# One DMA transpose per ds tile, and ten single ds buffers, in the backward loop of a fused attention and FFN kernel

## The chip, the cores and the metric

The kernel runs on one core of one Trainium2 chip. The metric is the device time of one execution in microseconds (us); lower is better. Most executions of one kernel lie within 0.3% of their median. "Ratio" is always the mean time of one kernel's fast runs over that of the kernel before in the same rounds on the same chip, so it is not quite the ratio of the medians that stand beside it.

## The reference, cut to what matters

The function is a transformer block with attention and a SwiGLU FFN in parallel; the kernel returns its output and the gradients of the input and of five weights.

```
xn  = layernorm(x)                                   # x: 2048 x 448, 16 heads of 28
out = x + attention(xn, wqkv, wo) + swiglu(xn, w_gate, w_up, w_down)
grads = vjp(out)(grad_out)
```

The attention backward needs, for every head and every tile of 128 queries by 512 keys, the matrix ds (the softmax weights times the gradient that reaches them). ds is used as it is for dk, and transposed for dq. How it gets transposed is what the change is about.

## The kernel before

The backward loop has 512 steps; a step treats one query tile of two heads. Four steps, qi = 0 to 3, make a block. In each step TensorE (PE) computes two score tiles and two gradient tiles, ScalarE (ACT) the exponentials and VectorE (DVE) the two products that are ds. In a block, the tiles 0 and 1 are transposed by one DMA as a pair, tile 2 by a DMA of its own, and tile 3 by PE. All these DMAs and, but for four stores at its start, all loads and stores of the loop are issued by SyncE (SP), one after the other.

```python
def dst_dma(b, ds, qi):                       # transposes by DMA, issued on SP
    if qi == 2:
        SP.dma_start_transpose(out=dsT[b][:, 2]..., in_=ds[:, 0]...)        # 8 tiles of 128 x 128
        return
    dsT[b] = bk.tile([P, 4, 2, 4, P], BF16, name="dsT", bufs=3)
    SP.dma_start_transpose(out=dsT[b][:, 0:2]..., in_=ds[:]...)             # 16 tiles: the pair

def ew(k):
    ...                                       # ACT: e_sb = exp(scores)
        if qi % 2 == 0:
            dss[k - 1] = dss[k] = kq.tile([P, 2, 2, 512], BF16, name="ds_sb", bufs=5)   # a pair
        ds = dss[k - 1]
        for j in range(2):
            DVE.tensor_tensor(out=ds[:, qi % 2, j], in0=dps.pop((k - 1, j))[:], in1=est[k - 1][:, j], op=ALU.mult)
        if qi == 1 or qi == 2 and b < NB // 4 - 1:
            ... dst_dma(b, ds, qi)

def tr_unit(b):                               # tile 3 by PE, at step 4b + 8
    ds = dss.pop(4 * b + 3)
    ...
def dq_unit(b):                               # PE, at step 4b + 13: reads dsT[b], all four tiles
    ...
def flush(upto):                              # stores of the loop, also on SP
    while held and held[0][0] <= upto:
        _, o, i = held.pop(0)
        SP.dma_start(out=o, in_=i)

for k in range(NB + 12):                      # cut
    row(k); ew(k)                             # PE rows, then ACT and DVE
    flush(k); drop()                          # stores due, loads due
    ...                                       # dk/dv matmuls, tr_unit, dq_unit, fill-in matmuls
```

A ds pair lives in one of five buffers, so DVE may start to rewrite it nine steps after the pair was complete, if its readers are done; the last of them is often the DMA transpose.

The softmax here doesn't subtract the row's maximum and nothing guards it: scores larger than these inputs give would overflow.

## Time and profile before

Runs gave a median of 1472.74 us (1466.82 to 1473.25).

| | us |
|---|---|
| span of the profiled execution | 1468.9 |
| backward loop (first ds product to the last, worked out from the trace) | 801.1 |
| PE idle in the loop (neither a matmul nor a weight load) | 52.3 |
| DVE waiting for a ds transpose | 15.9 |
| SP's issue time in the loop: 255 transposes | 561 |
| SP's issue time in the loop: 283 other DMAs (plain, but for one transpose of another tile) | 167 |

From the page of the kernel before: the span; busy time of the engines; and the group of the ds products (line, engine, operation, shapes, count, then busy us and mean ns, then idle us before it).

```profile
span 1468.9 us, 34341 instructions
...
PE 1338.7 (91%) x12647; PEld 544.8 (37%) x12708; DVE 1153.9 (79%) x1997; ACT 1262.4 (86%) x2193; POOL 361.8 (25%) x486
...
L845 DVE TENSOR_TENSOR ds_sb<-db,e_sb 128x512 bf16<-128x512 f32 x1024 | 648.4, 685 | 68.6 <-PE db L818 22.6
...
DMA packets 697664, 271.14 MB, mean 185 GB/s; under 512 B 616128, under 2 KB 672152, under 8 KB 697496
```

No engine is far ahead of the others, so a stall of any of them soon holds up PE. From the tile view of dsT: engine, operation and count of the two kinds of transpose, with shortest, median and longest duration of their issue in ns.

```profile
L830 SPq DMA_TRANSPOSE dsT<-ds_sb x128: 1746/3044/4773, 626.8 to 1419.8; - x128
...
L826 SPq DMA_TRANSPOSE dsT<-ds_sb x127: 1232/1252/2486, 629.8 to 1415.9; - x127
```

A pair keeps SP for 3.0 us in the median, but 1.75 at best. The timeline of SP (start, us, what it issued) in a bad stretch shows that SP never pauses:

```profile
657.27 1.43 SPq L800 DMA_DIRECT2D out_dram<-dqT  x2
658.80 2.03 SPq L826 DMA_TRANSPOSE dsT<-ds_sb  x1
660.92 0.52 SPq L800 DMA_DIRECT2D dqkvT_d<-dkv  x1
661.50 0.97 SPq L767 DMA_DIRECT2D h_c<-F_d  x2
662.57 3.27 SPq L830 DMA_TRANSPOSE dsT<-ds_sb  x1
665.88 1.06 SPq L800 DMA_DIRECT2D out_dram<-dqT  x2
667.04 1.24 SPq L826 DMA_TRANSPOSE dsT<-ds_sb  x1
```

The pair issued at 662.57 had been ready since 653.85 (the end of its last ds product): SP is 8.7 us late with it. It landed at 667.69, and the DVE timeline of the same stretch (in brackets: idle time before the instruction and what ended it) shows who had been waiting for that buffer:

```profile
662.79 2.52 DVE L845 TENSOR_TENSOR ds_sb<-db,e_sb 128x512 bf16<-128x512 f32 x4 [0.67 <-DMA dsT<-ds_sb]
667.82 2.49 DVE L845 TENSOR_TENSOR ds_sb<-db,e_sb 128x512 bf16<-128x512 f32 x4 [2.51 <-DMA dsT<-ds_sb]
```

The waits view adds these up (us in total, times, longest): DVE for the transposes, and PE for DVE.

```profile
PE db L818 <- DVE ds_sb L845: 18.7, 36, 2.7
...
DVE ds_sb L845 <- DMA dsT<-ds_sb: 15.9, 11, 2.5
```

### The profile page before, as it was taken

To read this page: it belongs to the slowest core of one execution; us is meant where nothing else is said; L and a number is where in the kernel's file an instruction comes from. 1 tells how busy PE (TensorE), PEld (TensorE's weight loads), DVE (VectorE), ACT (ScalarE), POOL (GpSimd) and SP (SyncE) were. 2 spreads that over 40 slices of the span, in tenths; PEclk is the share of its full clock that TensorE was granted. 3 is DMA by queue.
4 is the path that set the end of the run, shared out by engine and by line. 5 is a ranking of instruction groups with operands and counts; after the bars stand their busy time and mean duration, and the time that the engine had idled before them with its cause. 6 is when DMAs were issued, how large, how long until landed. Compare 5 with 4: busy or idle time off the path is not lost. (4 is left out here: it accounts for less than half of the span.)

```text
span 1468.9 us, 34341 instructions
## 1 busy us (share of the span) xinstructions
PE 1338.7 (91%) x12647; PEld 544.8 (37%) x12708; DVE 1153.9 (79%) x1997; ACT 1262.4 (86%) x2193; POOL 361.8 (25%) x486
## 2 busy tenths in 40 slices
PE   5889999989999999888899989999999999999996
PEld 2333333333333333333333433433343444344343
DVE  6667756656667767497888878888889999899988
ACT  5789988988989998687888879899989999888974
POOL 6464514553344444010001101101001011010005
PEclk9999999999999999998999999999999999999998
DMA  5797957696778685699999999999999999999961
GB/s 151 147 210 179 223 118 179 165 197 155 167 160 190 145 184 125 206 198 199 214 204 196 214 204 189 210 203 216 212 195 194 206 217 217 199 194 206 193 140 59
DMA packets 697664, 271.14 MB, mean 185 GB/s; under 512 B 616128, under 2 KB 672152, under 8 KB 697496
## 3 DMA queue, kind: packets, MB, share of 16 engines
q1 hardware_dynamic: 692520, 262.82, 86.7%
q0 software_dynamic: 3568, 5.83, 1.8%
q8 instruction: 100, 1.64, 0.5%
q14 instruction: 68, 0.56, 0.1%
q10 hardware_dynamic: 1408, 0.30, 0.1%
HBM read 65.04 MB, written 59.90 MB: 85 GB/s over the span
## 5 line engine op out<-in xcount | busy, mean ns | idle before, releaser
L845 DVE TENSOR_TENSOR ds_sb<-db,e_sb 128x512 bf16<-128x512 f32 x1024 | 648.4, 685 | 68.6 <-PE db L818 22.6
L837 ACT ACTIVATE e_sb<-sb 128x512 bf16<-128x512 f32 x1024 | 554.1, 609 | 60.3 <-PE db L818 43.8
L611 ACT ACTIVATE eT<-s_w 128x1024 bf16<-128x1024 f32 x256 | 263.7, 1030 | 48.6 <-PE s_ps L608 45.8
L613 ACT ACTIVATE eT<-s_ps 128x512 bf16<-128x512 f32 x512 | 280.2, 611 | 0.0
L818 PE MATMUL db<-kd,qd 32*128 32x512 bf16 x1024 | 239.9, 385 | 19.5 <-DVE ds_sb L845 18.7
L810 PE MATMUL sb<-kd,qd 32*128 32x512 bf16 x1024 | 210.9, 389 | 7.5 <-DMA qd<-QD_d 3.7
L964 POOL TENSOR_TENSOR dq_acc<-dq_acc,dq_st 128x256 f32<-128x256 f32 x64 | 46.4, 724 | 588.6 <-ACT dq_st L962 588.6
L905 ACT COPY dsT<-db 128x1024 bf16<-128x1024 bf16 x128 | 130.0, 1016 | 37.1 <-PE db L900 36.5
L922 PE MATMUL acc<-ds_sb,qd 128*32 128x512 bf16 x1024 | 161.4, 392 | 0.0
L918 PE MATMUL acc<-e_sb,qd 128*32 128x512 bf16 x1024 | 159.4, 392 | 1.3 <-DVE dw_o L527 1.3
L379 POOL TENSOR_TENSOR nn<-nn,ag 128x512 f32<-128x512 f32 x56 | 71.2, 1272 | 253.9 <-DVE ag L377 245.4
L608 PE MATMUL s_ps<-QQ,KK 32*128 32x512 bf16 x512 | 125.5, 385 | 3.9
L1132 PE MATMUL genb<-wguT,dau_c 128*128 128x448 bf16 x448 | 117.5, 355 | 6.3 <-ACT dq_st L962 3.8
L608 PE MATMUL s_w<-QQ,KK 32*128 32x512 bf16 x512 | 100.3, 387 | 13.2 <-ACT eT L611 10.2
L810 PEld LDWEIGHTS <-qd 32*128 32x128 bf16 x1024 | 48.3, 91 | 152.6 <-issue 140.6
L420 PE MATMUL gen<-xn_t,f_sp 128*128 128x448 bf16 x416 | 91.8, 354 | 2.6 <-DVE nn L394 1.7
L949 PE MATMUL genb<-dsT,kd 128*32 128x256 bf16 x2048 | 80.9, 279 | 3.5 <-DVE y L1084 1.8
L420 PEld LDWEIGHTS <-f_sp 128*128 128x128 bf16 x640 | 55.7, 98 | 76.4 <-issue 31.7
L900 PE MATMUL db<-ident_bf,ds_sb 128*128 128x128 bf16 x1032 | 82.1, 225 | 0.9 <-DVE ds_sb L845 0.9
L900 PEld LDWEIGHTS <-ds_sb 128*128 128x128 bf16 x1032 | 70.6, 101 | 28.6 <-issue 10.3
L450 PE MATMUL gen<-eT,VS 128*32 128x512 bf16 x1024 | 68.0, 382 | 6.0 <-DVE nn L394 3.8
L380 POOL TENSOR_TENSOR nn<-nn,tt 128x512 f32<-128x512 f32 x56 | 72.0, 1286 | 4.4
(163 smaller groups left out, 1872.0 us busy)
## 6 DMA issues: line engine op xcount, KB each, us to landing
F_d<-hda SPq DMA_DIRECT2D x56, 384.0 KB
dau_c<-F_d SPq DMA_DIRECT2D x56, 256.0 KB
h_c<-F_d SPq DMA_DIRECT2D x24, 256.0 KB
qd<-QD_d SPq DMA_DIRECT2D x24, 256.0 KB
dc<-dqkvT_d SPq DMA_DIRECT2D x12, 384.0 KB
dsT<-ds_sb SPq DMA_TRANSPOSE x255
wT_d<-wT_f SPq DMA_DIRECT2D x14, 256.0 KB
KD_d<-qk_sp SPq DMA_DIRECT2D x7, 512.0 KB
```

What stands on the lines that cost most here:

```text
L420: PE.matmul(ps[:, :D], lhsT=fsp[fc][:, t // 4, w, t % 4, :], rhs=rhs[:, t, :], start=(t == 0), stop=(t == NT - 1))
L608: PE.matmul(sp4[hh], lhsT=KK[g][r:r + HP, kt * P:(kt + 1) * P], rhs=QQ[g][r:r + HP, qsl], start=True, stop=True, tile_position=(r, 0))
L611: ACTE.activation(out=e2[0][:], in_=wide[:], func=ACT.Exp, scale=SCALE)
L613: ACTE.activation(out=e2[1][:, j], in_=sp4[2 + j], func=ACT.Exp, scale=SCALE)
L810: PE.matmul(s_ps[:], lhsT=qside[g, qc][r:r + HP, 0, qi * P:(qi + 1) * P], rhs=kside[g, kc][r:r + HP, 0, :], start=True, stop=True, tile_po ...
L818: PE.matmul(d_ps[:], lhsT=qside[g, qc][r:r + HP, 1, qi * P:(qi + 1) * P], rhs=kside[g, kc][r:r + HP, 1, :], start=True, stop=True, tile_po ...
L837: ACTE.activation(out=est[k][:, j], in_=sps.pop((k, j))[:], func=ACT.Exp, scale=SCALE)
L845: DVE.tensor_tensor(out=ds[:, qi % 2, j], in0=dps.pop((k - 1, j))[:], in1=est[k - 1][:, j], op=ALU.mult)
L900: PE.transpose(ps[:, c, :], ds[:, qi % 2, c // 4, (c % 4) * P:(c % 4 + 1) * P], ident_bf[:])
L905: ACTE.copy(out=o, in_=ps[:])
L918: PE.matmul(a[r:r + HP, :], lhsT=sp4[:, 1, r:r + HP], rhs=e[:, j, :], start=first, stop=last, tile_position=(0, r), skip_group_check=True)
L922: PE.matmul(a[r:r + HP, :], lhsT=sp4[:, 0, r:r + HP], rhs=ds[:, qi % 2, j, :], start=first, stop=last, tile_position=(0, r), skip_group_ch ...
```

## The change

Each of the tiles 0, 1 and 2 gets its own DMA transpose, issued as soon as DVE has made the tile, and ds is kept in ten buffers of one tile. The memory is the same. The core of the diff:

```diff
     def dst_dma(b, ds, qi):
-        if qi == 2:
-            SP.dma_start_transpose(out=dsT[b][:, 2]..., in_=ds[:, 0]...)
-            return
-        dsT[b] = bk.tile([P, 4, 2, 4, P], BF16, name="dsT", bufs=3)
-        SP.dma_start_transpose(out=dsT[b][:, 0:2]..., in_=ds[:]...)
+        if qi == 0:
+            dsT[b] = bk.tile([P, 4, 2, 4, P], BF16, name="dsT", bufs=3)
+        SP.dma_start_transpose(out=dsT[b][:, qi]..., in_=ds[:]...)
 ...
-            if qi % 2 == 0:
-                dss[k - 1] = dss[k] = kq.tile([P, 2, 2, 512], BF16, name="ds_sb", bufs=5)
-            ds = dss[k - 1]
+            ds = dss[k - 1] = kq.tile([P, 2, 512], BF16, name="ds_sb", bufs=10)
 ...
-            if qi == 1 or qi == 2 and b < NB // 4 - 1:
+            if qi < 2 or qi == 2 and b < NB // 4 - 1:
 ...                                          # readers index ds[:, j] in place of ds[:, qi % 2, j]
```

More of the change, by code (lines that the diff above doesn't have):

```diff
@@ L824, in dst_dma @@
     def dst_dma(b, ds, qi):
-        if qi == 2:
-            SP.dma_start_transpose(out=dsT[b][:, 2].rearrange("p j kt s -> p (j kt) s"),
-                                   in_=ds[:, 0].rearrange("p j k -> p (j k)"))
-            return
-        dsT[b] = bk.tile([P, 4, 2, 4, P], BF16, name="dsT", bufs=3)
-        SP.dma_start_transpose(out=dsT[b][:, 0:2].rearrange("p q j kt s -> p (q j kt) s"),
-                               in_=ds[:].rearrange("p q j k -> p (q j k)"))
+        if qi == 0:
+            dsT[b] = bk.tile([P, 4, 2, 4, P], BF16, name="dsT", bufs=3)
+        SP.dma_start_transpose(out=dsT[b][:, qi].rearrange("p j kt s -> p (j kt) s"),
+                               in_=ds[:].rearrange("p j k -> p (j k)"))
     def ew(k):
@@ L840, in ew @@
             b = (k - 1) // 4
-            if qi % 2 == 0:
-                dss[k - 1] = dss[k] = kq.tile([P, 2, 2, 512], BF16, name="ds_sb", bufs=5)
-            ds = dss[k - 1]
+            ds = dss[k - 1] = kq.tile([P, 2, 512], BF16, name="ds_sb", bufs=10)
             for j in range(2):
-                DVE.tensor_tensor(out=ds[:, qi % 2, j], in0=dps.pop((k - 1, j))[:], in1=est[k - 1][:, j], op=ALU.mult)
-            if qi == 1 or qi == 2 and b < NB // 4 - 1:
+                DVE.tensor_tensor(out=ds[:, j], in0=dps.pop((k - 1, j))[:], in1=est[k - 1][:, j], op=ALU.mult)
+            if qi < 2 or qi == 2 and b < NB // 4 - 1:
                 if bk is None:
@@ L895, in tr_unit @@
     def tr_unit(b):
-        ds = dss.pop(4 * b + 3)
         for qi in (3,) if b < NB // 4 - 1 else (2, 3):
+            ds = dss.pop(4 * b + qi)
             ps = ps_b.tile([P, 8, P], BF16, name="db", bufs=3)
             for c in range(8):
-                PE.transpose(ps[:, c, :], ds[:, qi % 2, c // 4, (c % 4) * P:(c % 4 + 1) * P], ident_bf[:])
+                PE.transpose(ps[:, c, :], ds[:, c // 4, (c % 4) * P:(c % 4 + 1) * P], ident_bf[:])
             o = dsT[b][:, qi].rearrange("p j kt s -> p (j kt) s")
@@ L913, in kv @@
         e = est.pop(k)
-        ds = dss[k] if qi == 3 else dss.pop(k)
+        ds = dss[k] if qi == 3 or k == NB - 2 else dss.pop(k)
         sp4 = qside[g, qc][:, 2:4, qi * P:(qi + 1) * P]
@@ L921, in kv @@
             r = HP * (2 * hp + j)
-            PE.matmul(a[r:r + HP, :], lhsT=sp4[:, 0, r:r + HP], rhs=ds[:, qi % 2, j, :],
+            PE.matmul(a[r:r + HP, :], lhsT=sp4[:, 0, r:r + HP], rhs=ds[:, j, :],
                       start=first, stop=last, tile_position=(0, r), skip_group_check=True)
@@ L1336, in dx_b @@
         ACTE.activation(out=t1, in_=ps, func=ACT.Identity, scale=rstd[:, t:t + 1], bias=sa)
-        t2 = kq.tile([P, 2, 512], FP32, name="ds_sb", bufs=5)[:, 0, :D]
+        t2 = kq.tile([P, 512], FP32, name="ds_sb", bufs=10)[:, :D]
         dy = dy2[t // 4][:, t % 4, :] if t < 8 else dy4[:, t - 8, :]
```

## The prediction

> # Prediction
>
> **What bounds the kernel now.** The change touches only the backward loop: 512 steps from about 620 to 1422 us of a 1468.9 us span, 1.57 us a step. In the windows view the engines are nearly level there: over 1000 to 1100 us PE 93.4, ACT 89.2, DVE 85.5 us busy.
>
> A hidden resource is the SP queue, which issues the DMAs. The tile view of dsT shows 128 transposes of a ds pair at a median 3.044 us of issue (1.746 to 4.773) and 127 of one ds tile at 1.252 us. Summing SP's DMA instructions in stretches of 50 us, it is issuing for 88 to 101% of the time from 650 to 1350 us. Pairs therefore leave late: from DVE's end of a pair to SP's start of its transpose pass 8 to 13 us at 660 to 700 us, about 8 us near 830 us, about zero after 1290 us. A ds buffer is rewritten nine steps (about 14 us) after its transpose could start, so where the lag is large DVE must wait: the waits view gives "DVE ds_sb <- DMA dsT" 15.9 us in 11 waits, half of it before 720 us. "PE db <- DVE ds_sb" (18.7 us) includes its echo.
>
> **What the change does.** Bytes, matmuls and DVE work stay. 128 pair issues become 256 single ones: 383 transposes instead of 255. A pair that found few DMAs outstanding took about 1.8 us, so two singles at 1.25 us cost SP about 0.7 us more there. With DMAs outstanding, pairs take 3.0 to 3.3 us, while a single right behind a pair mostly takes 1.25 us: I read the pair's extra time as waiting for room in the DMA rings, an inference. Two singles are then an estimated 2.5 to 3.1 us, 0 to 0.6 us less per four steps. The Trainium skill, page "DMA: Bandwidth & Descriptors", section "Rules for kernel authors", advises to coalesce small transfers; the unblocked case agrees (1.8 against 2.5 us), the blocked case need not.
>
> The first tile's transpose may start a step earlier, landing in about 3.5 us instead of 5.1 from issue, and every buffer has ten steps from that possible issue to its rewriting: 1.5 us more slack. Against this, a dsT buffer is claimed a step earlier, so the first transpose may wait on the dq matmuls three blocks back.
>
> **How much is critical.** Only the DVE waits on the transposes and their echo in PE: at most about 16 us (1.1%). I expect a third to a half to disappear and some to be given back where SP has more to issue: net about 4 us. Elsewhere a later landing is harmless: dq reads dsT about eleven steps after the tile was made.
>
> **Time:** 1468 us, 8 in 10 between 1450 and 1487. Faster by over 2%: 0.04; within 2%: 0.91; slower by over 2%: 0.05.
>
> **What would show it.** Tile view of dsT: 383 single issues, median 1.25 us; if blocking moves onto the second single, its mean is 1.5 us or more. Sum of transpose issue time: 561 us before, 480 to 590 after. Waits view: "DVE ds_sb <- DMA dsT" under 8 us. Groups view: DVE, ACT and PE busy within 1%. DMA packets and bytes unchanged.
>
> **What would make it wrong.** If each single keeps a ring wait, or 128 more instructions push SP past its capacity, lag rises everywhere and the time goes up by some per cent. If the lag lengthens steps (1.78 us around 700 us, 1.47 near 1150 us) beyond the waits credited to it, the gain could reach 25 us.

## The result, and the profile after

The changed kernel takes a median of 1451.63 us (1450.09 to 1452.04, 4 runs) against 1469.78 us (4 runs): ratio 0.9874, 95% interval 0.9843 to 0.9905. It is 1.3% faster, within the stated range but near its lower end; 4 us had been expected, 18 were measured.

The same lines of the page, of the changed kernel (its line 840 is line 845 of before):

```profile
span 1448.2 us, 34787 instructions
...
PE 1335.4 (92%) x12708; PEld 539.9 (37%) x12708; DVE 1151.7 (80%) x1997; ACT 1261.2 (87%) x2193; POOL 363.1 (25%) x486
...
L840 DVE TENSOR_TENSOR ds_sb<-db,e_sb 128x512 bf16<-128x512 f32 x1024 | 646.8, 684 | 54.7 <-issue 25.5
...
DMA packets 701763, 271.18 MB, mean 187 GB/s; under 512 B 620224, under 2 KB 676248, under 8 KB 701592
```

The work is the same on every engine; only idle time went. (The 61 matmuls that PE seems to have had fewer before are records missing from that trace, all of them ahead of the loop.) DVE's short gaps changed their label from "PE db" to "issue", not their size: 22.6 and 7.9 us before, 6.2 and 25.5 after, in the waits views. The waits that fell are those for the transposes. The tile view of dsT in the changed kernel:

```profile
L827 SPq DMA_TRANSPOSE dsT<-ds_sb x383: 1231/1267/3143, 624.3 to 1400.5; - x192
```

And its waits view:

```profile
PE db L818 <- DVE ds_sb L840: 6.4, 26, 0.6
...
DVE ds_sb L840 <- DMA dsT<-ds_sb: 5.0, 6, 1.7
```

SP's timeline in the same stretch shows loads and stores slipping in between single issues of 1.23 us, and some of 1.3 to 2.6 us:

```profile
657.14 1.23 SPq L827 DMA_TRANSPOSE dsT<-ds_sb  x1
658.43 0.57 SPq L767 DMA_DIRECT2D h_c<-F_d  x1
659.09 2.55 SPq L827 DMA_TRANSPOSE dsT<-ds_sb  x1
661.70 1.05 SPq L800 DMA_DIRECT2D out_dram<-dqT  x2
662.84 1.23 SPq L827 DMA_TRANSPOSE dsT<-ds_sb  x1
```

Of the 20.7 us between the two profiled spans, 16.7 lie in the loop (801.1 to 784.4); the rest (2.5 us ahead of the loop, where the code is the same, and 1.5 us in the tail) is within what runs differ by. The loop by stretches, worked out from the traces (loop time; SP's issue time on transposes; on plain DMAs; all in us; a stretch begins with the first ds product of its first step, so the sums differ by up to 2 us from the figures for the whole loop), with three of the experiments below beside the two kernels:

| | steps 0 to 159 | steps 160 to 319 | steps 320 to 511 |
|---|---|---|---|
| before | 264.0; 180.7; 65.4 | 249.3; 179.9; 52.0 | 288.5; 202.0; 48.4 |
| changed | 252.8; 164.2; 67.7 | 248.4; 175.5; 52.1 | 283.8; 206.1; 45.6 |
| e11: pairs, stores on POOL | 249.1; 184.4; 49.8 | 247.5; 191.5; 35.9 | 292.2; 213.3; 41.7 |
| e7: changed, tiny extra stores | 280.3; 159.8; 95.1 | 269.3; 168.7; 77.9 | 307.9; 198.3; 85.3 |
| e10: changed, stores on POOL | 250.6; 172.8; 57.8 | 246.0; 182.8; 36.8 | 283.8; 206.9; 39.7 |

Of the 16.7 us, 11.2 lie in the first 160 steps (8.9 in the control's profile), where SP has the most to issue for the time. SP is full there: its issue times and the short gaps between them (under 0.3 us) add up to 260 of the 264.0 us before, 250 of 252.8 after, 246 of 249.1 in e11 and 276 of 280.3 in e7. There its time on transposes fell by 16.5 us, or 0.41 us a block, of which the one more issue a block takes back some 0.1 us in a gap between issues. Over the whole loop the sum moved much less: 561 us before, 544 after, with some 13 us more of short gaps. So SP's time was saved just where it was short. The mean time from "ready" to "landed" fell from 8.9 us for a pair to 7.9 for its second tile, and the slowest tenth from over 13.9 to over 12.1 us, against the nine steps or 14.1 us after which a buffer was wanted again.

### The profile page after: what moved, and what is told of

Same layout as the page of the kernel before. It is cut to its first block, busy times and chain, and to the rows that moved or that the text cites. A ratio compares the mean times of both kernels' runs of the same rounds, so it can differ in the third digit from the quotient of the medians.

```text
span 1448.2 us, 34787 instructions
## 1 busy us (share of the span) xinstructions
PE 1335.4 (92%) x12708; PEld 539.9 (37%) x12708; DVE 1151.7 (80%) x1997; ACT 1261.2 (87%) x2193; POOL 363.1 (25%) x486
## 5 line engine op out<-in xcount | busy, mean ns | idle before, releaser
L840 DVE TENSOR_TENSOR ds_sb<-db,e_sb 128x512 bf16<-128x512 f32 x1024 | 646.8, 684 | 54.7 <-issue 25.5
L834 ACT ACTIVATE e_sb<-sb 128x512 bf16<-128x512 f32 x1024 | 555.0, 612 | 66.1 <-PE db L818 49.8
L818 PE MATMUL db<-kd,qd 32*128 32x512 bf16 x1024 | 236.1, 385 | 7.2 <-DVE ds_sb L840 6.4
L900 ACT COPY dsT<-db 128x1024 bf16<-128x1024 bf16 x128 | 130.2, 1017 | 14.1 <-PE db L895 13.5
L895 PE MATMUL db<-ident_bf,ds_sb 128*128 128x128 bf16 x1032 | 79.0, 220 | 1.1 <-DVE ds_sb L840 1.1
```

The lines of the kernel that those rows point to most:

```text
L818: PE.matmul(d_ps[:], lhsT=qside[g, qc][r:r + HP, 1, qi * P:(qi + 1) * P], rhs=kside[g, kc][r:r + HP, 1, :], start=True, stop=True, tile_po ...
L834: ACTE.activation(out=est[k][:, j], in_=sps.pop((k, j))[:], func=ACT.Exp, scale=SCALE)
L840: DVE.tensor_tensor(out=ds[:, j], in0=dps.pop((k - 1, j))[:], in1=est[k - 1][:, j], op=ALU.mult)
L895: PE.transpose(ps[:, c, :], ds[:, c // 4, (c % 4) * P:(c % 4 + 1) * P], ident_bf[:])
L900: ACTE.copy(out=o, in_=ps[:])
```

## The experiments

The change has three parts that could each be the cause: the granularity of the DMAs (theory G), the earlier start of the first tile's transpose (theory S), and the buffers (theory B). Behind G stands a further question, whether SP's time is what is scarce (theory Q) or whether a pair does harm whatever SP's load. "PE idle" and "loop" are worked out from each run's trace; "clock lost" is the span times (1 minus the mean granted TensorE clock), averaged over the fast runs. Runs were made on several chips; each ratio is to the kernel before on the same chip, where its median was 1469.50 us (a1, e1 to e3), 1467.83 (e7, e8), 1469.58 (e10) or 1469.61 (e11).

| run | median us | ratio (95%) | loop | PE idle | clock lost |
|---|---|---|---|---|---|
| before (11 runs beside the first four) | 1469.50 | 1 | 801.1 | 52.3 | 35.0 |
| changed, again (a1) | 1453.75 | 0.9892 (0.9875 to 0.9908) | 786.6 | 41.2 | 30.8 |
| e2: single DMAs, pair buffers | 1453.57 | 0.9890 (0.9872 to 0.9907) | 787.0 | 42.9 | 27.9 |
| e3: changed, both singles at the pair's time | 1454.35 | 0.9896 (0.9879 to 0.9913) | 787.1 | 41.7 | 28.0 |
| e1: pairs, six pair buffers | 1465.16 | 0.9972 (0.9958 to 0.9987) | 795.8 | 45.4 | 35.4 |
| e8: changed, twelve buffers | 1451.39 | 0.9873 (0.9847 to 0.9899) | 783.2 | 45.7 | 27.5 |
| e7: changed, 256 tiny extra stores | 1524.10 | 1.0383 (1.0358 to 1.0409) | 856.9 | 83.8 | 53.3 |
| e11: pairs, stores on POOL | 1453.55 | 0.9890 (0.9873 to 0.9906) | 788.1 | 47.5 | 24.7 |
| e10: changed, stores on POOL | 1443.81 | 0.9815 (0.9787 to 0.9844) | 779.7 | 40.1 | 24.1 |

### The control

> The changed kernel again, as the control on this chip for the other three. Every theory: 1450 to 1453 us, ratio to the kernel before 0.985 to 0.990. DVE waits on the transposes about 5 us in the waits view.

It came out as said: 1453.75 us. DVE's waits on the transposes were 3.1 us in its profile.

### Single DMAs from pair buffers

```diff
 # kernel before, dst_dma
-        if qi == 2: ...one tile...; else: ...the pair...
+        if qi == 0:
+            dsT[b] = bk.tile(...)
+        SP.dma_start_transpose(out=dsT[b][:, qi]..., in_=ds[:, qi % 2]...)
```

> The kernel before with its five pair buffers, but each tile of a pair transposed by its own DMA as soon as DVE has made it: the DMA half of the change alone. Theory G (granularity: single issues leave SP and land sooner because they do not stall on the DMA rings) expects nearly the whole gain, 1450 to 1456 us. Theory B (buffers: the gain is the extra step of slack and the separate release of ten buffers) expects little, 1464 to 1472 us. In between means both.

1453.57 us, the same as the changed kernel on the same chip. The DMA half of the change is all of it; the buffers add nothing that these runs can show.

### Both singles issued when the pair is complete

```diff
 # changed kernel, ew
-            if qi < 2 or qi == 2 and ...: dst_dma(b, ds, qi)
+            todo = [(dss[k - 2], 0), (ds, 1)] if qi == 1 else [(ds, 2)] if qi == 2 and ... else []
+            for d, q in todo: dst_dma(b, d, q)
```

> The changed kernel, but the first tile's transpose is issued only together with the second's, back to back, when the pair is complete. Theory G in its form 'two singles are cheaper than a pair whenever they leave' and theory B expect 1450 to 1455 us. Theory S (the gain is the earlier start of the first tile's transpose, which spreads the DMA work) expects most of the gain lost: 1462 to 1470 us.

1454.35 us. Two singles back to back, in the very place of the pair, keep the gain, so the earlier start is not the cause. Theory S falls. (e2 keeps the earlier start and e3 the finer buffers; no run here takes both away and keeps the single DMAs.) The two singles took 1.36 and 1.52 us of issue on average, 2.89 in sum against the pair's 3.01.

### Six pair buffers

```diff
-  ds_sb: bufs=5          # pairs
+  ds_sb: bufs=6          # gs and pr, scratch of the tail, moved into buffers of qd and kd, idle by then
```

> The kernel before with six pair buffers in place of five (room made by letting two scratch tiles of the tail, gs and pr, live in buffers of qd and kd that are idle by then): two steps more slack before a ds buffer is rewritten, DMA issues as before. Theory B expects the whole gain or more, 1445 to 1453 us, with the DVE waits on the transposes near zero. Theories G and S expect the waits on ds buffers to shrink but SP to stay late, and 1462 to 1470 us.

1465.16 us, a quarter of the gain. The waits view shows where part of the rest went. In the kernel before, PE never waited on record for dsT at line 949, the dq matmuls; with six pairs it does:

```profile
PE db L818 <- DVE ds_sb L845: 4.5, 20, 0.2
...
PE genb L949 <- DMA dsT<-ds_sb: 4.2, 3, 2.1
...
PEld L949 <- DMA dsT<-ds_sb: 1.3, 2, 0.8
...
DVE ds_sb L845 <- DMA dsT<-ds_sb: 0.5, 1, 0.5
```

DVE no longer waits (0.5 us), but the transposes are as late as ever (9.3 us from ready to landed, 14.05 us or more in the slowest tenth), and PE meets them instead. Here more buffers moved the wait for a late producer and did not remove it. In the first 160 steps SP's issue times stayed as they were (180.8 us of transposes, 64.3 of others, against 180.7 and 65.4), and the stretch took 260.4 us against 264.0. Theory B falls as the main cause.

### Twelve single buffers

> The changed kernel with twelve ds buffers in place of ten (room made as for the six pairs). With six pairs the DVE waits went and most of the time stayed, because PE's dq matmuls waited for late transposes instead. So little is expected: 1448 to 1454 us, DVE waits on the transposes at zero. A gain of over 4 us would say that buffers still matter once singles are used.

The edit is `bufs=12` in place of 10, with the same room made in the tail. 1451.39 us, ratio 0.9873: no gain beyond the changed kernel, as expected.

### More work for SP

```diff
 # changed kernel, ew
+            if bk is not None and qi % 2:
+                SP.dma_start(out=dummy[(k - 1) // 2], in_=ident_bf[0:1, :])      # 256 bytes
```

> The changed kernel with one tiny extra store (256 bytes) issued by SP every second step, 256 in all; by the durations of other small issues (0.4 to 0.6 us) an estimated 100 to 150 us more of SP issue time in a loop of 785 us, and almost no data. Theory Q expects a large loss: lag at its limit throughout, 1490 to 1580 us. If SP's time is not scarce (only landing or data rate counts), 1450 to 1460 us.

The median was 1524.10 us, 70 us above the changed kernel's control, for 93 us more of plain issue time in the loop (260 us against 167; the extra issues were shorter than estimated). They move next to no data. This is the direct test of whether SP's time is scarce, in a changed kernel: three quarters of the time it was given to do in addition came back in the kernel's time. In the first 160 steps, 27 us more of plain issues (95.1 against 67.7) made that stretch 27.5 us longer. DVE's waits on the transposes rose with it:

```profile
DVE ds_sb L841 <- DMA dsT<-ds_sb: 35.8, 34, 3.0
```

### All loads and stores from POOL

```diff
 # drop, have, flush
-            SP.dma_start(out=o, in_=i)
+            POOL.dma_start(out=o, in_=i)
```

> The kernel before (pairs, five pair buffers), but in the backward loop the plain loads and stores (about 280 issues, 167 us of SP's issue time) go out from the POOL queue, so SP issues only transposes there. Theory Q (SP's queue is the scarce resource: what the change gained is backlog on SP) expects the lag from the pair's end to its issue to fall from 3.5 us on average to about 1, and the whole gain without any change to the pairs: 1445 to 1458 us. If the pair itself is the harm whatever SP's load (its long occupation of the DMA rings delays everything), 1463 us or more. POOL's slower issue or late loads could add some us.

> The changed kernel with the same move of plain loads and stores to POOL. Theory Q expects little beyond the change, 1440 to 1452 us, and about the same time as the pairs with POOL loads: once SP is free, pair or single is no matter. The rival, pairs harmful in themselves, expects this one to stay at least 10 us ahead of the pairs with POOL loads.

Both expectations failed. (POOL did take longer over a plain DMA: 0.72 us in the median for those that load h_c in the run with singles, against 0.57 on SP in the kernel before.) With pairs the kernel took 1515.5 to 1563.8 us (ratio of its two fast runs 1.0358), with singles a median of 1493.69 us (1.0160). In the second one's profile the single issues took 1.9 us on average, against 1.4 in the changed kernel: with loads in a second queue the transposes themselves are issued more slowly, and the 167 us that SP no longer spends on plain DMAs are spent on longer transposes. In its first 160 steps the transposes alone took 249 us of issue in 268.7, where transposes and plain DMAs together had taken 232 in 252.8: the move did not relieve SP at all. What makes the transposes slower was not settled; but an issue's time is plainly not SP's own alone, and "SP's time" in this document includes whatever holds an issue up. The runs therefore could not test theory Q. They suggest that pairs suffer more than singles from a second stream of loads, but with two fast runs of one of them that is no more than a hint.

### Stores alone from POOL

> The changed kernel with only the stores of the backward loop (some 70 issues, about 45 us of SP's time) issued from POOL; the loads stay on SP. Moving loads too made transposes slower to issue and cost 43 us against the changed kernel. If it was the loads from a second queue that crowd the transposes out, this one loses little or gains a few us: 1440 to 1456 us. If any traffic from the second queue does it, 1456 to 1475 us.

> The kernel before (pairs, five pair buffers) with only the stores of the backward loop moved from SP to POOL: the counterpart of the changed kernel with the same move, and the cleaner form of the run in which loads and stores were moved together. On the changed kernel the move took 31 us off SP's issue time of plain DMAs (167 to 136 us), about what the stream measurement gives for singles in place of pairs (0.12 to 0.25 us a block, 15 to 32 us in 128 blocks). Theory Q (any relief of SP of that size does what the change did) expects 1446 to 1458 us. If the pairs are harmful in themselves, by arriving late as one lump, 1462 us or more, and the changed kernel with the same move stays 15 us or more ahead.

Only the line in flush was changed, in the changed kernel and in the kernel before. This relieves SP without a second stream of loads: SP's plain issue time in the loop fell from 167 to 136 us with singles, to 129 us with pairs. The pairs then take 1453.55 us, the change's time, with the pairs and the five buffers untouched. From the waits view:

```profile
PE db L818 <- DVE ds_sb L845: 13.4, 26, 4.8
...
DVE ds_sb L845 <- DMA dsT<-ds_sb: 10.9, 4, 5.0
```

Here too the gain lies in the first 160 steps (table of the stretches): 15.6 us of plain issues less and 3.7 us of transposes more, and the loop 14.9 us shorter. Later the pairs grow longer, by 23 us in the other 352 steps, which uses up the relief there; one wait of 5.0 us remains, and the last stretch is even 3.7 us longer. So there are two quite different ways of taking 12 to 14 us off SP's issue times in the stretch where it is behind, and each shortens that stretch by about as much. With e7, which does the opposite, that is what theory Q said; that a pair should do harm whatever SP's load does not fit e11. Nor were the DMA engines themselves at a limit, though the windows view shows them busy all the time (their mean busy share in the first 160 steps is 1.02 before, 1.07 after, 1.09 in e11 and 0.99 in e7): the same bytes moved at 203 GB/s before, 212 after and 216 in e11, and at 190 in e7, which added next to none. The changed kernel with its stores on POOL is the fastest of all, 1443.81 us, ratio 0.9815: about 0.6% to 0.8% better than the change alone and 1.9% better than before. In its first 160 steps the transposes grew and took back nearly all that the stores had freed (231 us of issue against 232), and the stretch is only 2 to 4 us shorter than in the changed kernel's two profiles (252.8 and 255.1): the two reliefs do not simply add.

### The disputed cost by itself

> The disputed cost by itself: a kernel that computes nothing (its outputs are zeros, so wrong on purpose) and issues transposes on SP in streams of 24 blocks: one of 16 tiles a block; two of 8; one 256 KB load, then 16 and 8 tiles; the same load, then 8, 8, 8; and both with two loads. First each size alone, waiting for its landing. Alone, I expect 1.8 us of issue for 16 tiles and 1.24 for 8, as the unblocked ones in the traces. In the streams, theory R (a 16-tile transpose does not fit the DMA rings and holds SP until half of it has drained, leaving a bubble afterwards) expects the period of a block with 16 and 8 to be 0.3 us or more above that with 8, 8, 8. If both are bound by the same data rate, the periods agree within 0.1 us, and the gain in the kernel is not in the stream's rate but in its order and delay.

```python
for name, loads, parts in (("pp", 0, (16,)), ("ss", 0, (8, 8)), ("lp", 1, (16, 8)), ("ls", 1, (8, 8, 8)),
                           ("mp", 2, (16, 8)), ("ms", 2, (8, 8, 8))):
    for n in range(24):                     # six buffers; DVE touches each result
        ...loads of 256 KB on SP, then a DMA transpose of each size in parts on SP
```

Its result is zeros and was reported wrong, as intended. It ran once, so its state is unknown; the granted clock was 1.00. Alone, with the landing awaited before the next (tile view of the pair in the measuring kernel; ns shortest, median, longest):

```profile
L144 SPq DMA_TRANSPOSE pair_alone<-z x8: 1318/1850/1913, 43.0 to 75.5; - x8
```

and the tile view of the single:

```profile
L144 SPq DMA_TRANSPOSE single_alone<-z x8: 1232/1232/1823, 77.4 to 101.8; - x8
```

In streams, the period of a block (from the starts of blocks 7 to 24):

| stream | transposes' mean issue, us | period, us |
|---|---|---|
| 16 | 2.44 | 2.55 |
| 8, 8 | 1.28, 1.33 | 2.77 |
| load, 16, 8 | 2.99, 1.30 | 5.06 |
| load, 8, 8, 8 | 1.24, 1.35, 1.37 | 4.81 |
| 2 loads, 16, 8 | 3.33, 1.30 | 5.90 |
| 2 loads, 8, 8, 8 | 1.24, 1.85, 1.35 | 5.77 |

SP's timeline in the streams with one load, first with 16 and 8, then with 8, 8, 8:

```profile
284.06 0.53 SPq L169 DMA_DIRECT2D l_lp<-src_d  x1
284.68 4.51 SPq L144 DMA_TRANSPOSE d_lp<-z  x2
289.28 0.53 SPq L169 DMA_DIRECT2D l_lp<-src_d  x1
289.91 4.36 SPq L144 DMA_TRANSPOSE d_lp<-z  x2
...
404.17 0.52 SPq L169 DMA_DIRECT2D l_ls<-src_d  x1
404.79 3.94 SPq L144 DMA_TRANSPOSE d_ls<-z  x3
408.83 0.53 SPq L169 DMA_DIRECT2D l_ls<-src_d  x1
409.47 4.01 SPq L144 DMA_TRANSPOSE d_ls<-z  x3
```

Without loads the pair is the cheaper form (2.55 against 2.77 us). Behind a load the order turns round: the pair grows from 2.44 to 3.0 or 3.3 us, the singles hardly, and a block of three singles is 0.25 us shorter with one load, 0.12 with two (the scatter from block to block gives standard errors of about 0.04 and 0.07 us, so the first is clear and the second barely). The theory that a pair is held up where singles are not had asked for at least 0.3 us; the sign is as it said, the size is smaller. For the 40 blocks of the first 160 steps that makes an estimated 5 to 10 us of SP's time, where 16.5 us less on transposes were measured: the stream shows the direction, not the whole size, and what in the kernel's own traffic adds the rest stays open. That the growth is a wait for room in the DMA rings is an inference: it fits that a single behind a pair is not held up, but no run shows the rings.

### Still smaller pieces

```diff
 # changed kernel, dst_dma
-        SP.dma_start_transpose(out=dsT[b][:, qi]..., in_=ds[:]...)
+        for j in range(2):
+            SP.dma_start_transpose(out=dsT[b][:, qi, j], in_=ds[:, j])
```

> The changed kernel with every tile's transpose cut once more, into two of 4 matrix tiles: 766 issues. The slope between the unblocked 8 and 16 (1.24 and 1.8 us) gives an estimated 0.97 us for 4, so six would take SP 5.8 us a block of four steps beside 1.4 us of loads: more than a block's 6.1 us. Theory Q+R (SP's time is scarce, and smaller pieces help only as long as the fixed part of an issue is smaller than the blocking that they avoid) expects a large loss, 1530 to 1620 us. If finer always means sooner, 1440 to 1455 us.

The median was 1900.95 us, ratio 1.2940, a much larger loss than expected. Its tile view says why:

```profile
L828 SPq DMA_TRANSPOSE dsT<-ds_sb x766: 1188/1216/2537, 621.7 to 1846.2; - x192
```

An issue of 4 tiles takes 1.22 us, as long as one of 8. My estimate of 0.97 us, drawn as a line through 8 and 16, was wrong: going from 8 tiles to 4 saves nothing. Six of them are 7.3 us a block, more than the whole block had (6.1 us). SP was full throughout this loop: 959 us of transposes, 164 of other DMAs and 87 of short gaps in 1219.6 us.

## Why the prediction was right or wrong

- **SP's queue as the hidden resource: right.** e7 (70 us for 93 us of extra issues) and e11 (16 us gained by taking the loop's stores off SP) show it, not the argument from occupancy alone. (Redone from the trace, the lag near 830 us is 6 to 7 us rather than 8, and from 1320 to 1335 us it is again 2 to 3.)
- **"0 to 0.6 us less per four steps" where SP is behind: right.** It was 0.41 us in the first 160 steps, less about 0.1 us for one more gap; the stream gives 0.12 to 0.25.
- **"The first tile's transpose may start a step earlier", "1.5 us more slack": true of the code, worth nothing in time that these runs can show.** e3 took the first away and e2 the second, and both kept the whole gain.
- **"At most about 16 us ... a third to a half to disappear and some to be given back ... net about 4 us": the step that failed.** DVE's waits fell by two thirds or more (15.9 to 5.0 and 3.1 us), PE's on DVE from 18.7 to 6.4 (8.6 in the control); nothing was given back, since the dearer issues fell where SP had time. More than that, the sum of the waits was not what to count. In the first 160 steps SP is full, and what a kernel saves or adds in SP's time comes back nearly whole in the time of the stretch: 14.2 us less of issue and 4 more of gaps made it 11.2 us shorter, 11.9 less of issue and 2 less of gaps made it 14.9 shorter in e11, and against the changed kernel 23 more of issue and 3 more of gaps made it 27.5 longer in e7; and with six pairs, where DVE's waits went and SP's time stayed, it kept 260.4 of 264.0 us. The range held all the same, but with 1.6 us to spare: it was wide enough for a gain of four to five times the expected one, which is some luck.
- **What PE lost besides waiting is open.** PE's idle time alone fell by 9 to 11 us. On average over a kernel's runs, PE's clock was lost for 35.0 us before, and for 24.3 (first runs) or 30.8 us (control) after. The windows view of the kernel before shows the pattern (PE, PEld, DVE, ACT, POOL busy, then the granted clock, DMA share and GB/s):

```profile
663.49:666.90 3.41, 2.29 (x23) 0.65 (x20) 1.82 (x3) 3.41 (x8) 0.72 (x1) 0.99 1.15 259
666.90:670.32 3.42, 1.74 (x12) 0.94 (x12) 2.49 (x4) 0.14 (x2) 0.00 (x0) 0.50 0.71 144
670.32:673.73 3.41, 3.41 (x37) 1.08 (x34) 1.29 (x2) 2.96 (x5) 0.00 (x0) 0.51 1.09 228
```

  At the end of the first stretch DVE begins to wait for the late pair, and PE is busy 2.29 of 3.41 us; in the next two the clock is halved. The Trainium skill, "TensorE: Matmul & The Clock Gate", Part 1, tells of such windows of about 3.4 us and of half clock after an idle one; the trace agrees on the 3.4 us (the half-clock periods last 3.41 or 6.83 us) and on the half, but the window before was far from idle. So a stall of PE may cost more than its own length. How much of the gain this is stays open: every kernel that lost less clock than the one before was also less idle, but with six pairs idle fell by 7 us, the clock lost stayed (35.4) and the time fell by 4. And in the loops of the profiled executions the clock lost was 16.9 us before, 10.5 after, but 17.1 in the control, whose loop was still 14.5 us shorter than before, 11 of them by less idle time. No run changed the clock alone.
- **"Elsewhere a later landing is harmless": nearly right for this change, not in general.** PE's dq matmuls waited 1.2 us for the transposes in the changed kernel and 0.2 in the control; with six pair buffers they became the ones that wait (4.2 and 1.3 us).
- **The checks named:** 383 issues, median 1.267 us, sum 544 us, second single no longer than the first (1.44 and 1.45 us on average), DVE's waits below 8 us, busy times within 1%: all as said. Bytes were equal; packets rose by 0.6%, not quite "unchanged".
- **The warning** that the lag could lengthen steps beyond the waits credited to it, with a gain up to 25 us, names what the first 160 steps then showed.

On the size of DMAs, the Trainium skill, "DMA: Bandwidth & Descriptors", section "Rules for kernel authors", advises to coalesce small transfers. Its small is under 64 KB, and 8 tiles are 256 KB, so no run here tests it in its own range. Taken further, it holds for transposes alone in the queue (2.55 against 2.77 us) and strongly for 4 tiles against 8 (1901 us), and no longer holds at 16 tiles behind loads (5.06 against 4.81 us).

## What to carry to other kernels

Look at how long the queue that issues the DMAs is busy and how long after "ready" it issues; a queue that never pauses is an engine like the others, and its lateness showed up here as short waits elsewhere, which more buffers only moved about. Test it with tiny extra issues, and by moving a few stores to an idle engine's queue: here that was worth as much as the change itself (16 us), and about 8 to 10 us more on top of it. The best size of a transpose was here not the largest that the data allow, but the largest that still went out at about its own issue cost in the traffic it met: 8 tiles (1.23 us alone, 1.27 in the loop), where 16 went from 1.85 to 3.04 us.

## What the Trainium skill lacked or had wrong

- "DMA: Bandwidth & Descriptors", section "Issuing engines are not separate DMA queues", says that issuing from several engines saves only the sequencer's time, "which is usually small relative to the DMA itself". For the pair transposes the issue took 3.04 us of 5.13 us from issue to landing (medians), and taking the loop's stores off SP gained 16 us with pairs and 8 to 10 us with singles. The same section does not warn that moving the loads as well can cost time: 1493.69 us against 1453.75.
- The same page has no issue time of a DMA transpose on this chip by its size (it has sequencer cycles of two transposes of "previous generations"). The runs show, in bf16, 1.22 us for 4 tiles of 128x128 in a full queue, 1.23 for 8 and 1.85 for 16 when alone, and 3.0 to 3.3 for 16 behind one or two loads.
- Its rule to coalesce has no upper end; here 16 tiles cost more than twice 8 tiles behind loads (a block of 5.06 against 4.81 us with one load).
- "TensorE: Matmul & The Clock Gate", section "Why this matters for your kernels", warns of idle gaps above about 3 us. In the loop of the kernel before, eight of the nine half-clock periods came after windows of 3.4 us with 1.05 to 2.43 us in all without a matmul, and one after 0.68; two windows with 1.12 and 1.20 us were not followed by one, nor, with twelve buffers, one with 1.84 us. So much shorter idle times than the page's can bring half clock, and no sharp limit comes out of these traces.
